# Packed attention feeding a soft mixture of experts on one core: a right-hand work space taken over early by five weight loads, one small product on another engine, and a rewritten order table

## The chip, the cores and the metric

One core of one Trainium2 chip runs the whole program. The metric is device time in microseconds (us), and less is better. Three runs of the kernel before took 237.82, 238.25 and 238.55 us; the median is 238.25 us.

## The reference, cut to what matters

```python
def sm_attn(qq, kk, vv):                       # scale = 1/sqrt(64)
    s = scale * (qq @ kk.T);  a = exp(s - max(s));  a = a / (sum(a) + 1e-9)
    return a @ vv
p_packed = sm_attn(p, k, v)                    # 32 packed rows read 576 keys, for each of 8 x 8 heads
out = sm_attn(q, p_packed, p_packed)           # 576 queries read the 32 packed rows
x = out.transpose(0, 2, 1, 3).reshape(4608, 512)
logits = x @ phi                               # 32 slots = 8 experts x 4
d = softmax(logits, over the 4608 rows)
slot_input = d.T @ x
slot_out[e] = relu(slot_input[e] @ w1[e]) @ w2[e]      # w1 512 x 1024, w2 1024 x 512, 8 experts
c = softmax(logits, over the 32 slots)
result = c @ slot_out                          # 4608 x 512, float32
```

All inputs are float32: q, k and v have 9.4 MB each, w1 and w2 16.8 MB each, p 0.5 MB, and the output 9.4 MB.

## The kernel before

The attention runs in eight steps (i = 0 to 7). A step takes two batches and four heads; two steps make a pair (dd = 0 to 3). In a step, VectorE transposes k (`kt`), TensorE makes the first scores (`s1`), VectorE takes their maximum (`mx1`) and ScalarE their exponential (`e1`). TensorE transposes the result (`ap`) and multiplies it with v (`m`); ScalarE and VectorE scale that (`ppa`, `pp`), and TensorE transposes the packed rows (`pt`). Meanwhile TensorE has transposed q (`qp`, copied out by `qc`) and now makes the second scores in two halves (`s2`, of 36 products each). VectorE takes their maximum and subtracts it (`mx2`, `sb`), ScalarE takes the exponential (`e2`), GpSimd sums and normalises (`z2`, `n2`), and TensorE transposes (`a2p`, copied out by `a2c`).

After each pair the logits follow (`lg`), and a running softmax over all rows: their maximum per slot (`f1` to `f4`), the exponential with its sum `zg` (`f5`, ScalarE), a transpose of that (`fd`, VectorE), `rw`, which is the 128x32 tile `rep` times `zg` (`f_rw`, L701, VectorE), the sum over partitions as a TensorE product with `rw` (`f6`, L706), the running sum `z_run` (`gz`), and the slots' weighted sum of the attention's output (`gr`, `rt`, `gt`, `rb`, `gs`, `sa`). `fl` (L696) keeps the logits for the end.

All of this is issued in the order of a table written out by hand, `ORDER`: each word names one piece, its step, its part, and after `@` the bank of the matmul accumulator (PSUM) and after `:` the engine of a copy. Each engine works through its own instructions in that order.

Loads go through one SyncE queue into a ring of 15.7 MB (`ring`, L129): `pump` (L151) issues the next load when its place is free, and `release` frees a place after the last reader. First p, then k, q, v of each step, then 32 MB of weights, in pieces of 1 MB. The work tiles of the attention lie in two pools, `dpool` on the left and `wpool` on the right. The word `late.0.0`, after the second scores of step 7, closes `wpool` and puts tiles of the last stage there (`f_late`, L797): `xz`, `hT`, `cT`, `identr`.

Then come the experts: `layer1a` (L861) multiplies the slots with w1 and releases each 1 MB piece after use, `layer2` (L917) does it with w2. Between them stand `cq` and `cp` (L933 to L951): nine groups of four transposes that bring the softmax over slots, split in two halves, into `cT`. After the last of them come the last expert (`last2`, L996), its sum, and the output: 36 products of `cT` with the slots' result, copied out by ScalarE and VectorE and stored.

## Time and profile before

| what | value |
|---|---|
| median of 3 runs | 238.25 us |
| the profiled execution | 237.79 us, span 236.0 us, mean granted clock 0.874 |
| TensorE busy | 182.5 us, 77% |
| VectorE busy | 126.1 us, 53% |
| ScalarE, GpSimd busy | 92.8 us, 47.4 us |
| HBM read and written | 62.46 MB, 9.44 MB |
| chain that ended last | TensorE 46%, DMA 17%, VectorE 17%, ScalarE 8% of the span |

Two lines of the page show the stages, in 40 slices of 5.9 us; a digit is the busy share in tenths:

```profile
PE   0987989999799995999997577899959655989000
...
DMA  7999999999999999922919000099999998019997
```

The DMA line is full for some 100 us (q, k, v and the first weights), nearly empty from about 130 to 153 us (the end of the attention), full again to 200 us (the rest of the weights), empty for 10 us, and full at the end (the output). TensorE is nearly full up to 88 us and has its loosest stretches where the DMA line is empty and where weights are awaited. A share of the whole span says little here; each stage has its own limit.

### The profile page before, as it was taken

How to read it: one execution, taken by the hardware profiler on the slowest of the kernel's cores; microseconds unless marked ns; L12 is line 12 of the kernel's file. 1: busy time of each engine (PE TensorE's matmuls, PEld its weight loads, DVE VectorE, ACT ScalarE, POOL GpSimd, SP SyncE). 2: the span in 40 equal slices, each digit the busy share in tenths (PEclk: the TensorE clock that was granted, in tenths of full speed). 3: DMA queues.
4: the chain of work that ended last, by engine and by line, in shares of the span. 5: the costliest groups of instructions: out<-in, count | busy, mean ns of one | idle time of the engine just before them, and what ended most of it. 6: DMA issues, size and time to landing. Idle time of an engine off the chain costs nothing.

```text
span 236.0 us, 6352 instructions
## 1 busy us (share of the span) xinstructions
PE 182.5 (77%) x2715; PEld 117.0 (50%) x2715; DVE 126.1 (53%) x248; ACT 92.8 (39%) x228; POOL 47.4 (20%) x76
## 2 busy tenths in 40 slices
PE   0987989999799995999997577899959655989000
PEld 0665858777496773486866533423311111457000
DVE  1785769676872886464757942772133022159200
ACT  0073847657568574347673422011100000059300
POOL 8100071535305344005458200000000000000000
PEclk9999999999999997799999675579995996599755
DMA  7999999999999999922919000099999998019997
GB/s 161 383 392 391 390 391 390 390 387 391 391 392 388 405 406 403 406 90 60 417 62 350 13 0 0 3 330 431 422 418 422 422 422 332 6 59 409 416 416 301
DMA packets 24683, 72.29 MB, mean 306 GB/s; under 512 B 4176, under 2 KB 4432, under 8 KB 22736
## 3 DMA queue, kind: packets, MB, share of 16 engines
q1 hardware_dynamic: 24080, 71.83, 79.0%
q8 instruction: 21, 0.34, 0.6%
q10 hardware_dynamic: 576, 0.07, 0.2%
q14 instruction: 6, 0.05, 0.1%
HBM read 62.46 MB, written 9.44 MB: 305 GB/s over the span
## 4 chain that ended last, share of the span: by engine, by line
PE 46%; DMA 17%; DVE 17%; ACT 8%; issue 2%; POOL 1%; POOLq 1%; ACTq 0%; DVEq 0%; SPq 0%
DMA ring<-in_moe_w_dram 15%; PE ps L355 6%; PE ps L408 5%; PE ps L868 4%; PE ps L498 4%; PE ps L526 4%; PE ps L1049 3%; PE ps L734 3%; PE ps L607 3%; DVE rw L701 3%; PE ps L386 3%; DVE kT L341 2%; ACT a L369 2%; DMA ring<-in_p_dram 2%; DVE a L557 2%
## 5 line engine op out<-in xcount | busy, mean ns | idle before, releaser
L920 PE MATMUL ps<-ring,hT 128*32 128x512 f32 x112 | 17.7, 722 | 9.4 <-DMA ring<-in_moe_w_dram 9.4
L583 POOL TENSOR_TENSOR zt<-a 128x576 f32<-128x576 f32 x7 | 9.9, 1408 | 72.2 <-ACT a L575 72.2
L341 DVE STREAM_TRANSPOSE kT<-ring 128x576 f32<-128x576 f32 x32 | 23.2, 754 | 1.0 <-DMA ring<-in_k_dram 1.0
L498 PE MATMUL ps<-ident,ring 128*128 128x128 f32 x144 | 20.4, 279 | 0.0
L526 PE MATMUL ps<-ppT,qT 128*64 128x64 f32 x576 | 18.5, 223 | 0.3 <-ACT mm L291 0.3
L598 POOL TENSOR_TENSOR a<-a,zs 128x1152 f32<-128x1152 f32 (+1 forms) x8 | 16.2, 2020 | 12.3 <-DVE zs L594 10.6
L291 ACT COPY qT<-ps 128x512 f32<-128x512 f32 (+1 forms) x43 | 17.9, 477 | 1.7 <-PE ps L498 1.3
L408 PE MATMUL ps<-ring,a1T 64*64 64x128 f32 x576 | 18.2, 272 | 0.3 <-ACT a1T L291 0.3
L291 ACT CAST cT<-ps 128x512 fp32r<-128x512 f32 x6 | 3.5, 586 | 37.1 <-PE ps L946 37.1
L526 PEld LDWEIGHTS ps<-ppT,qT 128*64 128x64 f32 x576 | 17.5, 138 | 0.7 <-ACT mm L291 0.4
L408 PEld LDWEIGHTS ps<-ring,a1T 64*64 64x64 f32 x576 | 15.8, 133 | 2.7 <-DVE rz L421 0.8
L868 PE MATMUL ps<-ring,xz 128*32 128x512 f32 x128 | 16.7, 678 | 0.4 <-DVE xz L953 0.4
L498 PEld LDWEIGHTS ps<-ident,ring 128*128 128x128 f32 x144 | 15.7, 141 | 2.5 <-issue 1.3
L355 PE MATMUL ps<-kT,pT 32*32 32x288 f32 x512 | 16.4, 446 | 0.7 <-issue 0.4
L366 DVE TENSOR_REDUCE nm<-ps 128x2 f32<-128x1152 f32 x8 | 10.9, 1356 | 10.3 <-PE ps L355 8.7
L549 DVE TENSOR_REDUCE mx<-ps 128x36 f32<-128x1152 f32 (+1 forms) x9 | 12.8, 1421 | 4.5 <-PE ps L526 3.4
L369 ACT ACTIVATE a<-ps,nm 128x576 f32<-128x576 f32 x16 | 11.8, 743 | 6.7 <-DVE nm L366 6.7
L607 PE MATMUL ps<-ident,a 128*128 128x128 f32 x72 | 11.9, 303 | 2.8 <-POOL a L598 1.4
L295 DVE CAST cT<-ps 128x512 fp32r<-128x512 f32 x3 | 2.1, 692 | 21.3 <-PE ps L946 21.3
L291 ACT COPY a1T<-ps 128x384 f32<-128x384 f32 x24 | 10.1, 487 | 6.3 <-PE ps L386 6.3
L291 ACT COPY a2T<-ps 128x384 f32<-128x384 f32 x23 | 10.0, 484 | 4.0 <-PE ps L607 4.0
L586 POOL TENSOR_TENSOR zt<-zt 128x288 f32<-128x288 f32 (+2 forms) x21 | 11.2, 535 | 1.6
(130 smaller groups left out, 286.1 us busy)
## 6 DMA issues: line engine op xcount, KB each, us to landing
ring<-in_moe_w_dram SPq DMA_DIRECT2D x31, 1024.0 KB, 13.7
ring<-in_k_dram SPq DMA_DIRECT2D x16, 576.0 KB, 11.9
ring<-in_q_dram SPq DMA_DIRECT2D x16, 576.0 KB, 11.9
ring<-in_v_dram SPq DMA_DIRECT2D x16, 576.0 KB, 12.0
out_dram<-ring SPq DMA_DIRECT2D x10, 768.0 KB, 8.3
ring<-in_moe_w_dram SPq DMA_DIRECT2D x2, 512.0 KB, 18.0
out_dram<-ring SPq DMA_DIRECT2D x2, 512.0 KB, 3.8
ring<-in_p_dram SPq DMA_DIRECT2D x1, 512.0 KB, 4.3
```

Of the source, the lines that this page charges most:

```text
L291: nc.scalar.copy(dst, src)
L341: nc.vector.transpose(kT[:, b2, :, c].rearrange("p m (t r) -> p m t r", t=T), view(f"k{i}.{b2}").rearrange("p (m t c d) -> p m t c d", m=2 ...
L355: nc.tensor.matmul(ps[32 * y : 32 * y + 32, z, 0 : 32 * T], pT[rs, dd, m, b2, g, c], kT[rs, b2, m, c], start=(c == 0), stop=(c == 1),)
L369: nc.scalar.activation(a1[:, :, x].rearrange("p t (h r) -> p h t r", h=2), s1v[:, x].rearrange("p h (t r) -> p h t r", t=T), AF.Exp, bias= ...
L408: nc.tensor.matmul(ps[64 * b2 : 64 * b2 + 64, b + x, 0:P].rearrange("p (m d) -> p m d", m=2), a1T[rs, t, b2], view(f"v{i}.{b2}").rearrange ...
L498: nc.tensor.transpose(ps[:, bank, o : o + P], view(f"q{i}.{b2}")[:, P * y : P * y + P], ident)
L526: nc.tensor.matmul(psf[64 * b2 : 64 * b2 + 64, o : o + 2 * NS].rearrange("p (u s) -> p u s", u=2), qT[:, b2, n, 64 * x : 64 * x + 64], col ...
L549: nc.vector.tensor_reduce(part(mxs[i % 2], c), s2v(i, c), axis=AX.X, op=ALU.max)
L598: (nc.vector if eng == "v" else nc.gpsimd).tensor_tensor(a, a, z.unsqueeze(3).broadcast_to([P, a.shape[1], a.shape[2], NS]), op=ALU.mult)
L607: nc.tensor.transpose(ps[:, bank, o : o + P], a2s[i // NG % 2][:, t, i % NG].rearrange("p c s -> p (c s)"), ident,)
L868: nc.tensor.matmul(ps[32 * a : 32 * a + 32, b + nh, :], xzf[:, (4 * e + a) * NSLOT : (4 * e + a + 1) * NSLOT], wv[:, j, nh * 512 : (nh + 1 ...
L920: nc.tensor.matmul(ps[32 * a : 32 * a + 32, SO, :], hTf[:, (NJ * e + j) * NSLOT : (NJ * e + j + 1) * NSLOT], w2v(e, j), start=(e == 0 and ...
```

## The change

The program makes these changes together:

- **Right-hand space.** `a2_0` and the two `ppT` tiles move from `dpool` to `wpool`. `late` now allocates `xz` and five tiles `ext` of 1 MB there, and issues the next five weight loads into them at once. `hT` and `identr` are made later in the left-hand space; `cT` takes the space of `ext` after `layer2(1)`.
- **Order of the experts.** All nine `cp` groups follow `layer2(1)`; from `layer2(2)` to `layer2(5)` two groups stand behind each expert, and none behind the last.
- **`rw`.** The VectorE product L701 goes; ScalarE makes it in `f_f5`, behind the exponential.
- **Head.** p is loaded in four quarters, the first ahead of k and the others behind k of step 0. GpSimd makes `sel` before the other constants, and a first exponential on ScalarE stands ahead of everything.
- **Second scores.** Each half has its own pair of banks; maximum and subtraction are made by halves in every step.
- **`gt`.** Its four products become eight, each over half the columns.
- **`ORDER`** is rewritten as a whole.

```diff
-mm.7.0:a s2.7.0@0 f5.2.0 n2.6.0:p fd.2.0 rw.2.0 s2.7.1 late.0.0
+f6.2.0 s2.7.1@4 mx2.7.1 gz.2.0 a2p.6.2@6 mx2.7.2 a2p.6.1@1 a2c.6.2:a
...
-    loads.append(("p", B * NG * D, p.rearrange("b (g h) s d -> (h s) (b g) d", g=NG)))
+    loads.append(("p0", 2 * NG * D, rows_p(0)))
     for i in range(NSTEP):
         for b2 in range(2):
             loads.append((f"k{i}.{b2}", 2 * T * D, rows9(k, i, b2)))
+        if i == 0:
+            for dd in range(1, ND):
+                loads.append((f"p{dd}", 2 * NG * D, rows_p(dd)))
...
+    first = const.tile([P, 1], F32, name="first")
+    nc.scalar.activation(first, ones[:, 0:1], AF.Exp)
...
-    a2s = [dpool.tile([P, T, NG, 4, NS], F32, name=f"a2_{x}") for x in range(2)]
+    a2s = [wpool.tile([P, T, NG, 4, NS], F32, name="a2_0"), a2_1]
...
-    ppTs = [dpool.tile([P, 2, 2, 4, NS], F32, name=f"ppT_{x}") for x in range(2)]
+    ppTs = [wpool.tile([P, 2, 2, 4, NS], F32, name=f"ppT_{x}") for x in range(2)]
...
-        if ("s2", i) not in banks:
-            banks["s2", i] = bank
-        b = 512 * banks["s2", i] + x * 2 * T * NS
+        if bank is not None:
+            banks["s2", i, x] = 512 * bank
+        else:
+            banks["s2", i, x] = banks["s2", i, 0] + 2 * T * NS
+        b = banks["s2", i, x]
...
+        nc.scalar.mul(rw, rep[:, 0], zg)
         if dd > 0:
             nc.scalar.activation(al, ps[:, b, W2 : W2 + NSLOT], AF.Exp)
...
-    def f_rw(dd, j, bank, eng):
-        nc.vector.tensor_scalar_mul(rw, rep[:, 0], zg)
...
         for a in range(4):
-            o = 2 * P + a * NSLOT
-            nc.tensor.matmul(
-                ps[:, b, o : o + NSLOT],
-                rt[:, a].rearrange("p b w s -> p (b w s)"),
+            for b2 in range(2):
+                o = 2 * P + a * NSLOT
+                nc.tensor.matmul(
+                    ps[64 * b2 : 64 * b2 + 64, b, o : o + NSLOT],
+                    rt[:, a, b2].rearrange("p w s -> p (w s)"),
...
-        hT = late.tile([P, E, NJ * NSLOT + SPE], F32, name="hT")
-        nc.gpsimd.memset(hT, 0.0)
-        cT = late.tile([P, NT, P], F32R, name="cT")
...
+        ext = [extp.tile([P, 2 * FF], F32, name=f"ext_{x}") for x in range(NEXT)]
...
+        for x in range(NEXT):
+            key, width, src = loads[state["next"]]
+            where[key] = (ext[x], width)
+            load(ext[x][:, 0:width], src)
+            state["next"] += 1
...
+    layer2(1)
+
+    ees.close()
+    lastp = ctx.enter_context(
+        tc.tile_pool(name="lastp", bufs=1, side="right", reuse_waits="tile")
+    )
+    cT = lastp.tile([P, NT, P], F32R, name="cT")
+    cp(0, "a")
+    for e in range(2, E - 1):
+        for n in range(2):
+            t0 = 8 * (e - 2) + 4 * n
+            if t0 + 4 < NT:
+                cq(t0 + 4)
         layer2(e)
+        for n in range(2):
+            t0 = 8 * (e - 2) + 4 * n
+            if t0 + 4 < NT:
+                cp(t0 + 4, "av"[n])
```

Three places in the order of the engines show what moves. Lines are those of each program; a row reads line, operation, output, inputs and shape.

The first place is the softmax over the rows after the second pair. On VectorE before, with `d` the transposed exponential, `zs` the sums that GpSimd normalises with, and `z_run` the running sum:

```order
L593 TENSOR_SCALAR zs_169<-zs_169 128x36
L594 RECIPROCAL zs_169<-zs_169 128x36
L691 STREAM_TRANSPOSE d<-rt 128x288
L701 TENSOR_SCALAR rw<-rep,zg 128x32
L714 TENSOR_TENSOR z_run<-z_run,al 128x32
L715 TENSOR_TENSOR z_run<-z_run,ps 128x32
```

and on ScalarE now:

```order
L320 COPY ppT_160<-ps 64x4x64 x2
L696 ACTIVATE nmg<-ps 128x1
L697 ACTIVATE rt,zg<-ps,nmg 128x288
L705 ACTIVATE rw<-rep,zg 128x32
L707 ACTIVATE al<-ps 128x32
```

The product left VectorE, where it stood behind the sums' reciprocal and the transpose, and stands right behind the exponential that makes `zg`.

The second place is TensorE at the same point. Before, `m` with its number and `dm` are the maximum and its step, `kT` the keys of step 5 and `a` the second attention's weights:

```order
L665 MATMUL ps<-ones,m_175 128x1
L673 MATMUL ps<-dm,ones 128x32
L498 MATMUL ps<-ident,ring 128x128 x4
L450 MATMUL ps<-ident,pp_147 128x128 x2
L498 MATMUL ps<-ident,ring 128x128 x2
L706 MATMUL ps<-rw,ones 128x32
L355 MATMUL ps<-kT,pT 32x288 x32
```

and now, where L542 are the second scores and L750 the weighted sum over rows:

```order
L683 MATMUL ps<-ones,m_185 128x1
L691 MATMUL ps<-dm,ones 128x32
L464 MATMUL ps<-ident,pp_157 128x128 x2
L542 MATMUL ps<-ppT_160,qT 64x64 x18
L722 MATMUL ps<-rw,ones 128x32
L486 MATMUL ps<-phi_sb,ppT_160 64x32 x4
L486 MATMUL ps<-phi_sb,ppT_161 64x32 x4
L542 MATMUL ps<-ppT_160,qT 64x64 x18
L750 MATMUL ps<-a_1_108,d 32x256 x18
```

The product with `rw` had eight transposes between it and the maximum's product; now half of a step's second scores stands there.

The third place is the SyncE queue of loads, around the last weights that are issued before the experts begin. Before:

```order
L167 DMA ring_73<-in_moe_w1_dram 128x2x1024 [waits DMAHW1_49,DVE_49,PE_49]
L167 DMA ring_73<-in_moe_w1_dram 128x2x1024 [waits DMAHW2_49,PE_49]
L167 DMA ring_73<-in_moe_w1_dram 128x2x1024 [waits DMAHW3_49,PE_49]
L167 DMA ring_73<-in_moe_w1_dram 128x2x1024 [waits DMAHW4_49,PE_49]
L167 DMA ring_73<-in_moe_w2_dram 128x2048 [waits DMAHW5_49,PE_49]
```

and now:

```order
L157 DMA ring_73<-in_moe_w1_dram 128x2x1024 [waits DMAHW5_49,PE_49]
L157 DMA ext_0_1891<-in_moe_w1_dram 128x2x1024 [waits DMAHW6_49,Activation_49]
L157 DMA ext_1_1892<-in_moe_w1_dram 128x2x1024 [waits DMAHW7_49,Activation_49]
L157 DMA ext_2_1893<-in_moe_w2_dram 128x2048 [waits DVE_49,DMAHW0_49,PE_49,Activation_49]
L157 DMA ext_3_1894<-in_moe_w2_dram 128x2048 [waits DMAHW1_49,PE_49,Pool_49]
L157 DMA ext_4_1895<-in_moe_w2_dram 128x2048 [waits DMAHW2_49]
L157 DMA ring_73<-in_moe_w2_dram 128x2048 [waits DMAHW3_49,PE_49]
```

In both programs 14 weight loads of 1 MB go into the ring before the experts. Then, before, the queue waits for `layer1a` to release a piece, with 18 MB to go; now five loads go to `ext`, waiting for the last readers and writers of the attention's tiles there, and 13 MB are left to wait for `layer1a`.

## Rows read from the trace of the kernel before

**Rows 1.** Two stretches: busy us (instructions) by engine, PEclk, DMA share, GB/s.

```profile
148.00:150.00 2.00, 1.41 (x12) 1.28 (x13) 0.91 (x4) 0.00 (x0) 0.00 (x0) 0.50 0.00 0
194.00:196.00 2.00, 1.06 (x8) 0.16 (x8) 0.00 (x0) 0.00 (x0) 0.00 (x0) 1.00 1.02 426
```

**Rows 2.** The chain that ended last: start, us, what.

```profile
176.86 19.83 DMA ring<-in_moe_w_dram
```

**Rows 3.** Timeline, experts: start, us, engine, line, instructions, [idle before <- releaser].

```profile
150.83 13.03 PE L868 MATMUL ps<-ring,xz 128*32 128x512 f32 x96 [0.45 <-DVE xz L953]
152.78 31.88 SPq L167 DMA_DIRECT2D ring<-in_moe_w_dram  x19
194.24 1.06 PE L920 MATMUL ps<-ring,hT 128*32 128x512 f32 x8 [0.95 <-DMA ring<-in_moe_w_dram]
196.73 1.86 PE L920 MATMUL ps<-ring,hT 128*32 128x512 f32 x8 [1.43 <-DMA ring<-in_moe_w_dram]
207.36 0.42 DVE L1015 COPY sos<-ps 128x256 f32<-128x256 f32 x1 [5.97 <-PE ps L997]
```

**Rows 4.** Timeline around L701, and line L423's view (ns min/median/max).

```profile
89.47 0.19 ACT L688 ACTIVATE al<-ps 128x32 f32<-128x32 f32 x1
90.20 2.12 POOL L598 TENSOR_TENSOR a<-a,zs 128x1152 f32<-128x1152 f32 x1 [0.77 <-DVE zs L594]
90.32 2.04 DVE L701 TENSOR_SCALAR rw<-rep,zg 128x32 f32<-128x32 f32 x1
...
125.96 3.45 DVE L701 TENSOR_SCALAR rw<-rep,zg 128x32 f32<-128x32 f32 x1
126.76 2.66 DVE L549 TENSOR_REDUCE mx<-ps 128x18 f32<-128x576 f32 x1
130.15 0.75 DVE L549 TENSOR_REDUCE mx<-ps 128x18 f32<-128x576 f32 x1
140.16 0.47 DVE L696 STREAM_TRANSPOSE L_sb<-ps 128x288 f32<-128x288 f32 x1
143.54 0.20 DVE L701 TENSOR_SCALAR rw<-rep,zg 128x32 f32<-128x32 f32 x1
...
L423 DVE TENSOR_TENSOR rzm<-rz,rm x8: 161/162/1059, 17.0 to 118.2; 128x4 f32<-128x4 f32 x8
```

**Rows 5.** TensorE's timeline, first and second pair's softmax over the rows.

```profile
60.05 1.60 PE L355 MATMUL ps<-kT,pT 32*32 32x288 f32 x64
62.84 0.38 PE L706 MATMUL ps<-rw,ones 128*128 128x32 f32 x2 [0.84 <-DVE rw L701]
63.15 1.49 PE L734 MATMUL ps<-a,d 64*32 64x256 f32 x36
92.51 0.60 PE L706 MATMUL ps<-rw,ones 128*128 128x32 f32 x2 [2.79 <-DVE z_run L714]
93.04 2.59 PE L355 MATMUL ps<-kT,pT 32*32 32x288 f32 x64
95.56 2.60 PE L734 MATMUL ps<-a,d 64*32 64x256 f32 x36
```

**Rows 6.** The head: the chain's first load, VectorE's second step, TensorE's second step.

```profile
0.74 4.35 DMA ring<-in_p_dram
...
19.61 0.78 DVE L341 STREAM_TRANSPOSE kT<-ring 128x576 f32<-128x576 f32 x1 [0.72 <-DMA ring<-in_k_dram]
...
21.72 1.60 PE L355 MATMUL ps<-kT,pT 32*32 32x288 f32 x64
```

**Rows 7.** The waits view of TensorE, 11.7 to 127 us: us in total, times, longest.

```profile
PE ps L450 <- DVE pp L437: 2.2, 4, 1.1
```

**Rows 8.** The timeline of the last expert's products.

```profile
201.58 1.94 PE L997 MATMUL ps<-ring,hT 128*32 128x256 f32 x16
203.45 2.08 PE L1010 MATMUL ps<-sot,rep 128*128 128x256 f32 x4
```

**Rows 9.** The timeline: one of the nine groups of transposes between the experts.

```profile
187.79 0.53 PE L946 MATMUL ps<-identr,c 128*128 128x128 f32 x4
```

More of the change, by code (lines that the diff above doesn't have):

```diff
@@ L15 @@
 RING = 30 * 4096
+NEXT = 5
 ORDER = """
[L20 to L26 removed]
@@ new lines @@
+lg.2.0@7 ppa.7.1 z2.6.0:p ppa.7.0 pp.7.1 qp.7.4@6 pp.7.0 f1.2.0
+qp.7.0@3 qc.7.4:a f2.2.0 qp.7.3@2 qc.7.0:v qp.7.1@6 qc.7.3:a f3.2.0
+qp.7.5@3 qp.7.2@1 pt.7.0 qc.7.1:a qc.7.5:a qc.7.2:a ptc.7.1:v ptc.7.0:a
+f4.2.0 rc.6.0 mp.7.0 f5.2.0 s2.7.0@2 n2.6.0:p mm.7.0:v fd.2.0
+f6.2.0 s2.7.1@4 mx2.7.1 gz.2.0 a2p.6.2@6 mx2.7.2 a2p.6.1@1 a2c.6.2:a
+a2p.6.0@0 sb.7.1 a2c.6.1:a a2c.6.0:a gr.2.0@2 late.0.0 sb.7.2 fl.2.0
+e2.7.3 e2.7.4 z2.7.3:v rt.2.1:a rt.2.0:a rc.7.3 gt.2.0 z2.7.4:v
+n2.7.3:p rc.7.4 rb.2.0 n2.7.4:v gs.2.0 a2p.7.0@7 sa.2.0 a2p.7.1@6
@@ L144, in view, with load @@
     def view(key):
-        off, width = where[key]
-        return ring[:, off : off + width]
+        place, width = where[key]
+        return ring[:, place : place + width] if isinstance(place, int) else place[:, 0:width]
+    def load(dst, src):
+        shape = src.shape[1:]
+        if len(shape) == 2:
+            dst = dst.rearrange("p (a b) -> p a b", a=shape[0])
+        elif len(shape) == 3:
+            dst = dst.rearrange("p (a b c) -> p a b c", a=shape[0], b=shape[1])
+        nc.sync.dma_start(out=dst, in_=src)
     def free(off, width):
@@ L160, in pump @@
             where[key] = (off, width)
-            dst = ring[:, off : off + width]
-            shape = src.shape[1:]
-            if len(shape) == 2:
-                dst = dst.rearrange("p (a b) -> p a b", a=shape[0])
-            elif len(shape) == 3:
-                dst = dst.rearrange("p (a b c) -> p a b c", a=shape[0], b=shape[1])
-            nc.sync.dma_start(out=dst, in_=src)
+            load(ring[:, off : off + width], src)
             state["next"] += 1
@@ L535, in s2v @@
     def s2v(i, c):
-        o = 512 * banks["s2", i]
+        o = banks["s2", i, 0 if c != 2 else 1]
+        if c in (1, 2):
+            return psf[:, o : o + 2 * T * NS].rearrange("p (a t s) -> p a t s", a=2, t=T)
         f = psf[:, o : o + 4 * T * NS].rearrange("p (a t s) -> p a t s", a=4, t=T)
@@ L751, in f_gt, with f_w @@
         for a in range(4):
-            o = 2 * P + a * NSLOT
-            nc.tensor.matmul(
-                ps[:, b, o : o + NSLOT],
-                rt[:, a].rearrange("p b w s -> p (b w s)"),
-                rep[:, 0],
-                start=True,
-                stop=True,
-            )
+            for b2 in range(2):
[3 more added lines that the diff above has]
+                    rt[:, a, b2].rearrange("p w s -> p (w s)"),
+                    rep[:, 0],
+                    start=True,
+                    stop=True,
+                )
+    def f_w(n, j, bank, eng):
+        for _ in range(n):
+            nc.tensor.transpose(ps[:, bank, 0:P], ident, ident)
     def f_rb(dd, j, bank, eng):
```

187 lines of the change are left out of this document (87 added, 100 removed).

## The prediction

> **What bounds the kernel now.** I read the chain of waits first, then the windows, then the timeline of each stage. The chain says which stage ends on what: in its last stretch before the output it is one DMA piece of 19.83 us, a load of weights [rows 2]. The windows say what else those stages could use: from 148 to 150 us, at the end of the attention, the DMA engines move nothing and TensorE's granted clock is 0.50, the lower of its two levels (1.2 GHz); from 194 to 196 us the DMA share is 1.02, the clock is 1.00 and TensorE works for 1.06 of 2 us [rows 1]. So there are three stages with different limits: the attention up to 150.83 us, a chain through all compute engines; the experts from there to the end of the last expert's products at 207.36 us, limited by loads [rows 3]; and the rest to 236.0 us, 28.64 us, limited by the stores of the output.
>
> **Stage 2, the five loads.** The queue issues its next weights 1.95 us after the first expert's product (152.78 against 150.83), and 19 loads follow, 17 of 1 MB and two of half that [rows 3]. The sixteenth lets the product at 196.73 start; the one before it stands at 194.24, so a piece takes 2.49 us, and 196.73 - 152.78 - 16 x 2.49 = 4.1 us lie ahead of the first [rows 3]. Five pieces less leave 13 MB: 1.95 + 4.1 + 13 x 2.49 = 38.4 us after the start of stage 2. What hides the five loads is the end of the attention: from the last step's second scores (their maximum starts at 126.76 [rows 4]) to 150.83 are 24 us, in which the DMA engines have nearly nothing else, and five pieces need 12.5 us. If that cover were gone, they would come back at 2.49 us each. On SyncE's queue they stand ahead only of loads that must wait for the experts anyway, so their own waits for the attention's tiles hold up nobody.
>
> Behind the last load come products. At the lower clock the halves of the last expert take 1.94 us each, with 2.08 between them [rows 8]. The twelfth piece lands at 38.4 - 2.5 = 35.9; 35.9 + 1.94 + 2.08 + 1.94 = 41.9 us. At the upper clock each of these halves, and the load sets the end: 38.4 + 0.5 = 38.9. Eight records took 1.06 us at 194.24 and 1.86 at 196.73 after the same kind of wait [rows 3], so both levels occur; I take the middle, 40.4 us, and keep both ends. Before, this stage took 207.36 - 150.83 = 56.5 us: the gain is 16.1.
>
> TensorE has to keep pace: 128 records of w1 at 13.03/96 are 17.4 us, seven experts' w2 at twice 1.06 are 14.8 [rows 3], and nine groups of transposes at 0.53 are 4.8 [rows 9], together 37.0, against 38.4 for the loads. The groups cost nothing as long as that holds; it is close, and it is a rival below.
>
> **Stage 1, the product on ScalarE.** In the second pair the VectorE product started at 90.32 and took 2.04 us; GpSimd's normalisation started at 90.20, took 2.12, and the two end within 0.04 us of each other [rows 4]. In the third pair the product took 3.45, in the fourth, with GpSimd idle, 0.20 [rows 4]. So it is held until GpSimd is done. TensorE waited for it 0.84 us in the first pair and 2.79 in the second, and came out of the second wait at half its pace: 2.59 instead of 1.60 us for the scores, 2.60 instead of 1.49 for the weighted sum [rows 5]. In the third pair the maximum behind it took 2.66 us instead of 0.75 [rows 4], on the chain that ends the attention. Together 0.84 + 2.79 + 0.99 + 1.11 + 1.91 = 7.6 us. A ScalarE operation of the same shape takes 0.19 [rows 4], three of them 0.6: the gain is 7.0 if the product's own wait is not replaced. Next late is `zg` itself, and half of a step's second scores now stands between on TensorE.
>
> Against this move speaks a sentence of the Trainium skill, page Perfetto Trace Analysis, section Optimizing Scalar/DVE Operations: "If a DVE performance mode (2x or 4x) is available, it will be faster". By that sentence alone the move gains nothing and the sum below is 218.0; the rows have 0.20 against 0.19 us alone and 2.04 to 3.45 beside GpSimd, so by them it is 211.0. (The same section warns of a port that GpSimd and VectorE share, and with that the rows agree.)
>
> **Stage 1, the head.** The first load takes 4.35 us on the chain, and a quarter of it now goes ahead; that bounds the gain from above at three quarters, 3.3 us. But the k of step 1 keeps its place in the queue: VectorE waits for it until 19.61, two transposes of 0.78 follow, and the scores that need them start at 21.72 [rows 6], so at that point only 21.72 - 21.17 = 0.55 us can be gained. Step 2 is less tied to its loads. I take the middle, 1.9. The early exponential loads ScalarE's table beside the first load: nothing.
>
> **Stage 1, the rest of the order.** TensorE waits 2.2 us for the scaled packed rows before transposing them [rows 7]; now the next step's scores, 1.60 us long [rows 5], stand ahead of that transpose in several steps. Between 0 and 2.2 I take 1.5. The transpose of the logits (0.47, on the last pair's chain between two maxima [rows 4]) moves behind: 0.5. The second scores' maxima by halves take 0.75 each [rows 4]; a half can start earlier, and an extra instruction can be in the way. Either is worth at most 0.75 us in each of seven steps, so between 5.3 gained and 5.3 lost; I take nothing, since VectorE is busy about half of the time. The eight products of `gt` load as many columns as the four did: nothing; if eight more records cost 0.19 each, half of the 0.38 for two [rows 5], 1.5 in the last pair, where nothing covers them. The other edits move no work onto the path.
>
> Sum for stage 1: 7.0 + 1.9 + 1.5 + 0.5 = 10.9 us; the experts start at 139.9.
>
> **Sum.** 139.9 + 40.4 + 28.6 = 208.9 us of span. The profiled execution has 237.79 - 236.0 = 1.8 us around its span: 210.7. It lies 0.46 us under the median of the runs shown, so on that scale I forecast 211.1, and say 211.0 us.
>
> **The rivals.**
>
> - **The hold passes on.** GpSimd's normalisation still runs beside VectorE, and the operations behind the departed product stay there. For this: L423, two small tiles multiplied, took 1.06 us at its worst and 0.16 in the median [rows 4], so L701 is not the only one that is held. Against it: in the new order GpSimd's normalisation is mostly over when the running sum is formed. If all of the 7.0 us and the 1.5 of the transposes come back, 219.5. The Trainium skill, SBUF - State Buffer, section SBUF: two separate sides, has a rule for this: a VectorE operation with two inputs in SBUF is held while GpSimd reads SBUF; the row of L423 agrees.
> - **TensorE becomes the bound of the experts.** Its 37.0 us above are at 1.06 us for eight records; at 1.86, seven experts take 26.0 instead of 14.8 us [rows 3]. If half of them run so, 5.6 us: 216.6. It decides once TensorE needs more than about 40 us. For it: the clock fell at 196.73. Against: TensorE would wait less between pieces than now.
> - **The loads do not come early.** If the tiles' last readers come late or the queue is behind, all five fall into stage 2: 12.4 us, 223.4. Against: 24 us are free for 12.5 us of loads.
> - **The other side: a wait in every step.** Place: the second scores, whose halves now have bank pairs of their own, which transposes must leave. Price: if TensorE runs dry there as at 92.51, it loses 2.79 us and then 2.1 us at the lower clock [rows 5], 4.9 us a step. From six steps on (6 x 4.9 = 29) the gain of 27 is gone; in all eight it would be 39 lost, and the kernel at 250. Against: the maxima take 0.75 a half, and other work of TensorE stands between.
>
> **How the numbers follow.** The forecast gets 0.60, with a range of its own from 206.5 to 217: 1.4 + 0.7 + 1.5 below (head, transposes, clock) and 1.4 + 1.5 + 1.5 + 1.5 above (with `gt`). The hold passes on: 0.18. TensorE the bound: 0.13. Loads late: 0.05. A wait in every step: 0.02. The remaining 0.02 is for halves that gain up to 5.3, to 205.7. The range from 205.5 to 218.5 takes in the forecast, TensorE as the bound, and a hold that comes back in part; it leaves out the full return, late loads and the last rival. A measurement of this kernel can tell 0.3%, about 0.7 us, from no change. Faster 0.97, the same 0.01, slower 0.02.
>
> **What would show it.** Right: the loads into `ext` start near the end of step 7's second scores and land before the first w1 product; 14 loads follow that product, at 2.5 us per MB; the DMA line has no empty stretch of 20 us before the experts; `rw` takes 0.2 us in all four pairs and TensorE's wait for L706's successor is gone; the first w1 product starts near 140 us and the span after the last expert is still 28 to 29 us. Wrong: that product starts after 145 us; loads into `ext` land behind it; w2 products that start without waiting for a load; TensorE at clock 0.5 in the middle of the attention.

## The result, and the profile after

The changed kernel takes **216.66 us** (median of 4 runs, 214.71 to 218.41) against 238.03 us for the kernel before on the same chip: a ratio of 0.9035, with a 95% interval from 0.899 to 0.908. Forecast were 211.0 us, between 205.5 and 218.5. The sign and the range held; the forecast was 5.7 us too low. Ratios and intervals, here and below, come from undisturbed executions alone, so a ratio need not be the quotient of two medians. The profiled execution, the fastest of the four, took 214.71 us, 212.9 of them span, against 210.7 and 208.9 forecast for it.

The three stages show where: the attention up to the first w1 product, the experts up to the copy of the last expert's products, and the rest.

| stage | before | forecast | after |
|---|---|---|---|
| attention, to the first w1 product | 150.83 | 139.9 | 146.47 |
| experts, from there to the copy (L1015, now L1050) | 56.5 | 40.4 | 37.6 |
| the rest | 28.6 | 28.6 | 28.8 |

The page of the changed kernel:

```profile
span 212.9 us, 6420 instructions
...
PE 167.8 (79%) x2747; PEld 112.9 (53%) x2747; DVE 136.1 (64%) x286; ACT 85.2 (40%) x206; POOL 47.4 (22%) x75
...
PEclk9999999999999999999999999679999999999655
DMA  6999999999999999669919799941999999169996
...
q8 instruction: 21, 0.34, 0.7%
...
PE 47%; DMA 17%; DVE 14%; ACT 8%; issue 5%; SPq 0%; ACTq 0%; DVEq 0%
```

The stretch of nearly 25 us in which the DMA line was empty before the experts has shrunk to two slices of 5.3 us (digits 4 and 1). VectorE is busier (64% against 53%). And 5% of the chain of waits is now "issue", time for which the profile shows no other cause.

SyncE's queue in the timeline of the changed kernel answers to the 19 loads of [rows 3]:

```profile
122.94 7.31 SPq L157 DMA_DIRECT2D ext<-in_moe_w_dram  x5
147.55 18.82 SPq L157 DMA_DIRECT2D ring<-in_moe_w_dram  x14
```

The five loads go out while the attention's last step drains, and 14 instead of 19 follow the first w1 product, 1.08 us behind it. By the trace's DMA packets the five have landed by 142.4 us, 4 us ahead of that product. On the chain of waits the stretch before the output, against the one DMA piece of [rows 2], is now:

```profile
146.47 3.67 PE ps L889 x32
150.14 9.83 DMA ring<-in_moe_w_dram
160.03 20.84 DMA ring<-in_moe_w_dram
180.91 1.07 PE ps L1032 x16
```

TensorE's timeline around both ends of the experts, and VectorE's copy there:

```profile
140.40 0.41 PE L722 MATMUL ps<-rw,ones 128*128 128x32 f32 x2 [1.32 <-ACT al L707]
...
144.39 0.66 PE L770 MATMUL ps<-rep,rt 128*64 128x32 f32 x16 [0.93 <-DVE rt L324]
...
146.47 1.08 PE L889 MATMUL ps<-ring,xz 128*32 128x512 f32 x8 [0.45 <-DVE xz L974]
...
178.42 1.07 PE L941 MATMUL ps<-ring,hT 128*32 128x512 f32 x8 [0.81 <-DMA ring<-in_moe_w_dram]
180.91 1.07 PE L1032 MATMUL ps<-ring,hT 128*32 128x256 f32 x16 [1.43 <-DMA ring<-in_moe_w_dram]
```

```profile
184.09 0.42 DVE L1050 COPY sos<-ps 128x256 f32<-128x256 f32 x1 [3.85 <-PE ps L1032]
```

TensorE waits for weights at two places only, at 178.42 and 180.91. The windows of the experts (columns: the stretch; us busy and records of PE, PEld, DVE, ACT and POOL; granted clock; DMA share; GB/s) say why:

```profile
146.50:160.00 13.50, 13.50 (x132) 4.81 (x136) 7.90 (x12) 1.75 (x2) 0.00 (x0) 1.00 0.86 340
160.00:170.00 10.00, 10.00 (x98) 3.87 (x88) 4.82 (x16) 1.76 (x3) 0.00 (x0) 1.00 1.02 423
170.00:184.00 14.00, 11.59 (x107) 4.59 (x105) 5.87 (x17) 1.76 (x3) 0.00 (x0) 1.00 0.85 348
```

TensorE is busy for 35.1 of 37.5 us at the upper level of its clock, 2.4 GHz (granted clock 1.00); it ends at 184.05, and the last weights land at 182.9 us by the trace's DMA packets. Both limits are met within 1.2 us of each other. [rows 1] had a clock of 0.50 at 148 us.

The waits of TensorE from 6 to 146.4 us (us in total, times, longest), against [rows 4, 5, 7]:

```profile
PE ps L422 <- issue: 4.4, 3, 2.2
PE ps L802 <- DVE rb L786: 2.3, 2, 1.8
PE ps L770 <- DVE rt L324: 1.8, 2, 0.9
PE ps L369 <- DVE kT L355: 1.5, 2, 1.0
PE ps L722 <- ACT al L707: 1.3, 1, 1.3
...
PE ps L369 <- issue: 0.8, 1, 0.8
...
PE ps L542 <- issue: 0.2, 1, 0.2
```

The waits for `rw`, for `d` and for the scaled packed rows `pp`, which the forecast wanted gone, are gone. But **5.4 us of "issue"** stand at the top; the kernel before had 0.44 us. TensorE's timeline has them in the middle of rows of equal products:

```profile
28.10 0.54 PE L422 MATMUL ps<-ring,a1T 64*64 64x128 f32 x9
30.10 1.97 PE L422 MATMUL ps<-ring,a1T 64*64 64x128 f32 x63 [1.47 <-issue]
...
36.56 0.72 PE L369 MATMUL ps<-kT,pT 32*32 32x288 f32 x16 [0.82 <-issue]
...
46.30 0.87 PE L422 MATMUL ps<-ring,a1T 64*64 64x128 f32 x20
49.32 0.43 PE L422 MATMUL ps<-ring,a1T 64*64 64x128 f32 x4 [2.15 <-issue]
```

No semaphore is awaited there. The trace also records every transfer of queue q8, which the page calls "instruction": 21 of them, 0.34 MB, so 16 KB each. Counting all records of TensorE's queue (weight loads, products and 41 semaphore and drain instructions) from zero, the waits stand 256 records or a multiple of that apart, at 193 + 256 k, and each ends 1.2 to 1.5 us after the k-th transfer of q8 has landed:

```
 k   transfer of q8, us   wait before record   TensorE goes on, us   wait, us
 2     27.73 to 28.82             705                30.10             1.47
 3     33.95 to 35.04             961                36.56             0.82
 5     46.76 to 47.88            1473                49.32             2.15
13     97.94 to 98.92            3521               100.16             0.23
14    106.58 to 107.69           3777               109.14             0.82
```

So q8 brings TensorE's instructions, 256 at a time, and TensorE at times runs out of them. That is **theory A** of the experiments: freed time cannot be used where the next block of instructions is not there yet. From 27 to 92 us, with the DMA engines full, these transfers came 4.9 us apart or more in every kernel that loads all of q, k and v, mostly 6.1 to 6.5. The fetch of block k is not made long ahead: in the changed kernel, for k from 3 to 12, it started 2.7 to 3.9 us after TensorE had begun the block before, at record 193 + 256 (k - 1). The rivals are **B**, VectorE has become the bound of the attention, and **C**, GpSimd or ScalarE hands its hold on.

### The profile page after: what moved, and what is told of

Same layout as the page of the kernel before. It is cut to its first block, busy times and chain, and to the rows that moved or that the text cites. A ratio compares the mean times of both kernels' runs of the same rounds, so it can differ in the third digit from the quotient of the medians.

```text
span 212.9 us, 6420 instructions
## 1 busy us (share of the span) xinstructions
PE 167.8 (79%) x2747; PEld 112.9 (53%) x2747; DVE 136.1 (64%) x286; ACT 85.2 (40%) x206; POOL 47.4 (22%) x75
## 4 chain that ended last, share of the span: by engine, by line
PE 47%; DMA 17%; DVE 14%; ACT 8%; issue 5%; SPq 0%; ACTq 0%; DVEq 0%
DMA ring<-in_moe_w_dram 14%; PE ps L422 7%; PE ps L542 7%; PE ps L369 6%; PE ps L512 6%; PE ps L400 4%; ACT ring L320 3%; DVE a L575 3%; PE ps L625 3%; DMA ring<-in_k_dram 3%; DVE mx L567 2%; PE ps L335 2%; PE ps L750 2%; PE ps L889 2%; ACT a L593 2%
## 5 line engine op out<-in xcount | busy, mean ns | idle before, releaser
L422 PE MATMUL ps<-ring,a1T 64*64 64x128 f32 x576 | 19.7, 274 | 4.4 <-issue 4.4
L542 PE MATMUL ps<-ppT,qT 128*64 128x64 f32 x576 | 20.1, 224 | 2.2 <-ACT ppT L320 1.0
L542 PEld LDWEIGHTS ps<-ppT,qT 128*64 128x64 f32 x576 | 18.2, 138 | 4.1 <-issue 2.7
L369 PE MATMUL ps<-kT,pT 32*32 32x288 f32 x512 | 16.3, 446 | 2.3 <-DVE kT L355 1.5
L567 DVE TENSOR_REDUCE mx<-ps 128x18 f32<-128x576 f32 x16 | 11.9, 746 | 5.5 <-PE ps L542 5.5
L320 ACT COPY qT<-ps 128x512 f32<-128x512 f32 (+1 forms) x32 | 14.0, 486 | 3.6 <-PE ps L512 3.5
L380 DVE TENSOR_REDUCE nm<-ps 128x2 f32<-128x1152 f32 x8 | 10.9, 1358 | 6.1 <-PE ps L369 6.1
L889 PE MATMUL ps<-ring,xz 128*32 128x512 f32 x112 | 12.5, 593 | 0.4 <-DVE xz L974 0.4
L575 DVE TENSOR_TENSOR a<-ps,mx 128x576 f32<-128x576 f32 x16 | 11.9, 754 | 0.3
L593 ACT ACTIVATE a<-a 128x1152 f32<-128x1152 f32 (+2 forms) x9 | 9.5, 1062 | 6.5 <-DVE a L575 6.5
L369 PEld LDWEIGHTS ps<-kT,pT 32*32 32x32 f32 x512 | 7.3, 107 | 8.2 <-issue 2.8
L941 PE MATMUL ps<-ring,hT 128*32 128x512 f32 x88 | 10.9, 599 | 0.8 <-DMA ring<-in_moe_w_dram 0.8
L400 PE MATMUL ps<-ident,a 128*128 128x128 f32 x72 | 10.0, 277 | 1.1 <-ACT a2T L320 0.7
```

Source lines behind the costliest of these rows:

```text
L320: nc.scalar.copy(dst, src)
L369: nc.tensor.matmul(ps[32 * y : 32 * y + 32, z, 0 : 32 * T], pT[rs, dd, m, b2, g, c], kT[rs, b2, m, c], start=(c == 0), stop=(c == 1),)
L400: nc.tensor.transpose(ps[:, bank, o : o + P], a1[:, t].rearrange("p x r -> p (x r)"), ident)
L422: nc.tensor.matmul(ps[64 * b2 : 64 * b2 + 64, b + x, 0:P].rearrange("p (m d) -> p m d", m=2), a1T[rs, t, b2], view(f"v{i}.{b2}").rearrange ...
L542: nc.tensor.matmul(psf[64 * b2 : 64 * b2 + 64, o : o + 2 * NS].rearrange("p (u s) -> p u s", u=2), qT[:, b2, n, 64 * x : 64 * x + 64], col ...
L567: nc.vector.tensor_reduce(part(mxs[i % 2], c), s2v(i, c), axis=AX.X, op=ALU.max)
```

## The experiments

The times below belong to single profiled executions and are for the first w1 product, the experts, and the sum of the "issue" waits; the medians and ratios (to the kernel before on the same chip) come from all runs. One more execution of the unchanged new kernel (the last experiment) gives 147.24 and 40.87 us where the first gave 146.47 and 37.62; differences under 1 us in the attention, or under 3 us in the experts, are not read as effects. The same program has the ratios 0.904 and 0.923 in two series of runs, with intervals that do not meet, so ratios of different series are not compared more closely than that. The kernels with product and loads, with the head added, with `gt` whole and the whole change once more ran in one series, on one chip.

| kernel | first w1 | experts | issue | median | ratio (95%) |
|---|---|---|---|---|---|
| before | 150.83 | 56.5 | 0.4 | | |
| before, product on ScalarE | 144.95 | 54.8 | 1.1 | 229.67 | 0.965 (0.957 to 0.973) |
| product and loads | 146.16 | 41.5 | 1.3 | 217.28 | 0.919 (0.907 to 0.931) |
| product, loads, head | 148.60 | 39.3 | 1.3 | 217.79 | 0.925 (0.919 to 0.932) |
| whole change | 146.47 | 37.6 | 5.4 | 216.66 | 0.904 (0.899 to 0.908) |
| whole change, once more | 147.24 | 40.9 | 3.9 | 216.81 | 0.923 (0.914 to 0.931) |
| without the product's move | 151.32 | 39.5 | 5.0 | 221.07 | 0.930 (0.923 to 0.937) |
| without the early loads | 146.32 | 53.9 | 4.6 | 232.65 | 0.977 (0.969 to 0.985) |
| with the old order | 150.81 | 41.1 | 3.1 | 221.89 | 0.943 (0.934 to 0.952) |
| with gt whole | 149.98 | 40.3 | 3.2 | 219.80 | 0.933 (0.922 to 0.943) |

### The product alone, and the change without it

To the kernel before, in `f_f5` behind the exponential (`f_rw` does nothing):

```diff
+        nc.scalar.mul(rw, rep[:, 0], zg)
```

> The kernel before with one part of the change: rw's product goes to ScalarE, right behind the exponential of its pair; order, head and loads are as before. The prediction's sum gives this part 7.0 us (median 231.0, four waits of TensorE on L706 gone). Theory A (up to some 90 us TensorE is held by its instruction fetch, because the loads fill the DMA engines, so time freed there comes back as a wait called issue): the waits of pairs 0 and 1 lie in that stretch and their 3.6 us are given back, so about 3.4 us are left, median 234.6. Theory B (VectorE has become the bound of the attention): a product less on VectorE shows whole, 7 us or more, 231 or under.

To the changed kernel, out of `f_f5` and into `f_fd` behind the transpose:

```diff
-        nc.scalar.mul(rw, rep[:, 0], zg)
+        nc.vector.tensor_scalar_mul(rw, rep[:, 0], zg)
```

> The changed kernel with rw's product back on VectorE, behind the transpose of d; all else as changed. The prediction's sum: 7.0 us slower, median 223.7. Theory A: pairs 0 and 1 cost little, since TensorE has issue waits there anyway; about 3.4 us slower or less, 218 to 220. Theory B: 7 us slower or more.

Alone on the kernel before, the move brings the first w1 product 5.9 us earlier and the median to 229.67 us. Taken out of the whole change it costs 4.1 to 4.9 us at that place (against the two executions of the unchanged kernel), and the median is 221.07 us. The prediction's 7.0 was near. Theory A, as stated for the first of these runs, was not: the wait of pair 1 did not come back, and the median is the one that B gave (231 or under); the second lies between A and B. In the second run the product on VectorE is held once only, 1.45 us in the third pair against 0.19 to 0.22 in the others, and TensorE waits for it 2.2 us in all; what the rest of the 4.1 to 4.9 us is was not settled. The instructions of `rw` and of VectorE in pair 1, in the kernel with the product alone (the first row: ns min, median and max, first and last start):

```profile
L687 ACT ACTIVATE rw<-rep,zg x4: 321/322/324, 62.2 to 138.3; 128x32 f32<-128x32 f32 x4
```

```profile
90.50 0.42 DVE L692 STREAM_TRANSPOSE d<-rt 128x288 f32<-128x288 f32 x1
90.84 2.06 DVE L715 TENSOR_TENSOR z_run<-z_run,al 128x32 f32<-128x32 f32 x1
93.00 0.19 DVE L716 TENSOR_TENSOR z_run<-z_run,ps 128x32 f32<-128x32 f32 x1
```

ScalarE takes 0.32 us in all four pairs. VectorE's next operation with operands in SBUF is held instead, 2.06 us beside GpSimd's normalisation (90.72 to 92.84): the rival "the hold passes on" happens in this kernel once. It did not cost the gain, since TensorE does not wait for `z_run` as it did for `rw`. In the whole change no operation of VectorE on such small tiles takes more than 1.13 us (a copy of 128x128, at 62.37).

### The five loads

To the changed kernel:

```diff
-NEXT = 5
+NEXT = 0
```

> The changed kernel without the five early loads (their number set to 0; the places of the other tensors stay). The prediction's sum: the loads are worth 12.4 us of the experts, so about 229. Rival: the loads carry all of the 18.9 us by which the experts got shorter, so 235.6. Both leave the attention's end (first w1 product) where it is, near 146.5; if it moves, loads and attention meet.

The attention ends where it did (146.32), and the experts take 53.9 instead of 37.6 to 40.9 us: the loads are worth 13.0 to 16.3 us in the profiles, 16 in the medians, between the two expectations. TensorE's waits from 146 to 201 us in this kernel:

```profile
PE ps L941 <- DMA ring<-in_moe_w_dram: 9.0, 9, 1.4
PE ps L1032 <- DMA ring<-in_moe_w_dram: 1.0, 1, 1.0
```

Ten waits for weights, against two with the loads. In between, TensorE's clock falls. The windows of the same kernel:

```profile
170.00:180.00 10.00, 7.15 (x52) 2.57 (x56) 2.81 (x9) 1.17 (x2) 0.00 (x0) 0.83 1.01 421
...
190.00:200.20 10.20, 7.78 (x52) 2.45 (x44) 0.69 (x1) 0.00 (x0) 0.00 (x0) 0.67 0.54 220
```

### Is the late fetch caused by the loads?

Three kernels change the loads of q, k and v and nothing that TensorE does. The first holds at most two steps' loads in the ring (in `pump`):

```diff
+AHEAD = 12
...
+            if key[0] in "kqv" and sum(r[0][0] in "kqv" for r in regions) >= AHEAD:
+                return
```

> The changed kernel, with at most 12 loads of q, k and v (two steps) held in the ring at a time, so that these loads follow the work instead of filling the DMA engines up to 90 us. Theory A: the fetches of TensorE's instructions come in time, its issue waits of about 5 us between 28 and 110 us go, and the first w1 product comes 3 to 6 us earlier (140.5 to 143.5 instead of 146.5), median 211 to 214. Theory B (VectorE is the bound) and theory C (GpSimd or ScalarE hands its hold on): no earlier than 146 us, median 216 to 217, or later if loads are missed.

The second makes each load of q, k and v in two halves (in `load`):

```diff
-        nc.sync.dma_start(out=dst, in_=src)
+        if src.shape[-1] == T * D:
+            c = T * D // 2
+            for y in range(2):
+                nc.sync.dma_start(out=dst[:, :, y * c : y * c + c], in_=src[:, :, y * c : y * c + c])
+        else:
+            nc.sync.dma_start(out=dst, in_=src)
```

> The changed kernel with each load of q, k and v as two DMAs of half the columns (pieces of 1152 B instead of 2304 B), a remedy if a fetch waits behind pieces of loads. Theory A with that mechanism: fetches come about 5 us apart instead of 6.2, issue waits fall from 5.4 us to under 2.5, first w1 product at 143 to 144.5 us, median 213 to 215. If the fetch waits behind bytes or behind its own latency, nothing moves: 146.5 and 216 to 217.

Neither helped: first w1 product at 147.38 and 149.45 us, issue waits 4.1 and 4.2, medians 218.03 us (ratio 0.916, 0.909 to 0.923) and 220.82 us (0.940, 0.930 to 0.950). The first did not do what it was meant to: q, k and v landed 12.0 us after their issue as before, and the DMA line stayed full. The second moved 357 GB/s where the whole loads move 390, and the fetches came no closer. For k from 3 to 12 they started 3.05 us on average after TensorE had begun the block before, against 3.45 us in the changed kernel, so halving the pieces does not halve a fetch's wait; for the rest these two decide nothing.

The third takes the loads away, of the changed kernel and of the one before. Steps 2 to 7 go from the list of loads and read the places of steps 0 and 1, which are not released before the end:

```diff
+        return key[0] + str(int(key[1]) % 2) + key[2:] if key[0] in "kqv" else key
...
+            if key[0] == "w" and state.get("used", 0) < 30:
+                return
...
```

> The changed kernel, but steps 2 to 7 read the q, k and v of steps 0 and 1 again and load nothing (their data is left out), and the weights' loads wait until 30 of the 48 pieces are used up, so that the DMA engines are idle from about 20 us to 90 us while the instructions stay the same. Theory A (instruction fetches of TensorE stand behind the loads): the issue waits of 5.4 us go to under 1 us from 25 us on, fetches come less than 6 us apart where TensorE asks for them, and the first w1 product comes at about 141 to 142.5 us. Theory B (VectorE is the bound): waits on VectorE take their place and the first w1 product stays at 145.5 to 146.5 us.

> The same edit on the kernel before: steps 2 to 7 read the q, k and v of steps 0 and 1 again, no loads between about 20 and 90 us. It has 0.44 us of issue waits, so theory A expects 0.4 to 1 us: first w1 product at 150 to 150.4 us instead of 150.83. If it comes 3 us earlier or more, then the loads cost both kernels something besides the fetch (VectorE's and ScalarE's accesses, or TensorE's own).

The page of the changed kernel with this edit, and two rows of TensorE's timeline:

```profile
DMA  6999999800000005000587699704999997069996
```

```profile
30.12 1.97 PE L436 MATMUL ps<-ring,a1T 64*64 64x128 f32 x63 [1.47 <-issue]
...
36.30 0.72 PE L383 MATMUL ps<-kT,pT 32*32 32x288 f32 x16 [0.55 <-issue]
```

The ring still fills up to about 43 us, so the first two waits are there. From then on the DMA engines are idle, and **no issue wait is left**: the 2.15 us at 49 us and the two behind 97 us are gone. The starts of the fetches (us), and the time at which TensorE began the block before each, tell the same:

```
                          k = 3      4      5      6      7
changed kernel          33.95  40.37  46.76  53.08  60.51
  block before begun    30.10  36.56  42.93  49.32  57.61
without the loads       33.88  40.00  43.57  47.32  55.11
  block before begun    30.12  36.30  42.47  46.54  54.78
```

Beside full DMA engines a fetch starts 2.7 to 3.9 us after the block before it is begun (k from 3 to 12), with idle engines at most 1.1 us after (k from 5 to 13). How far apart the fetches then come is TensorE's own pace: 3.6 and 3.8 us where it catches up, 7.8 us at k = 7. The first w1 product comes at 143.91 us, 2.6 us earlier, of 3.2 us of issue waits removed; that is between the two expectations. At the `gt` products of the third pair it is 3.8 us ahead (126.63 against 130.41 us); 1.2 us of that are lost in the last pair, where its granted clock is 0.50 for 11.1 us up to the first w1 product, against 6.8 us. B and C are out as the cause: VectorE, ScalarE and GpSimd have the same work in both. On the kernel before, the same edit moves that place by 0.7 us (150.16; ratio 0.999, 0.993 to 1.005), as A expects of a kernel with hardly any such wait. (The median of the first, 215.66 us, is not comparable: its weights come later, and its experts take 41.6 us.)

The waits can cost more than their own time. In the changed kernel's second execution the clock falls 2.0 us after the wait that ends at 48.55 us, and stays down for 6.8 us:

```profile
50.60:57.40 6.80, 6.16 (x45) 5.54 (x49) 3.69 (x9) 4.52 (x13) 0.00 (x0) 0.50 1.05 388
```

From that wait's end to the second scores behind it are 9.66 us, against 6.96 us in the first execution, whose clock stayed at 1.00: 2.7 us. In five of the seven executions with this order and all loads the granted clock falls to 0.50 within 3 us of such a wait, for 3.4 to 6.8 us; the other two have waits as long without it.

### The order and the head

To the changed kernel, the whole order list of before (without `rw`, and with `late.0.0` behind `gr.2.0`):

```diff
-p.0.0 px.0.0@7 kt.0.0 pc.0.0:a kt.0.1 kt.0.2 kt.0.3 p.1.0
...
+p.0.0 p.1.0 px.0.0@7 p.2.0 p.3.0 px.1.0@6 pc.0.0:v kt.0.0 kt.0.1
...
```

> The changed kernel (product on ScalarE, p in four loads, the five early loads, the tensors' new places) with the order list of before; only rw's step is gone from it and the early loads stand behind the last sums of pair 2. Theory A (the new order packs TensorE's instructions so that its instruction fetch is late three to four times, 5.4 us of issue waits): under the old order these waits are about 1 us, and the first w1 product comes at 143 to 145 us as with the product alone on ScalarE (144.95), against 146.5 under the new order; experts 37.6 us, median 213 to 215. Rival (the 5.4 us missing are lost to the new code or the places of the tensors, whatever the order): first w1 product at 148 or later, median 218 or more.

The first w1 product came at 150.81 us: the number of the rival. But the two tables don't differ alone here. The old one asks for all four quarters of p before the first scores, and three of them now arrive behind k; the first scores start at 14.79 us, not at 11.74. So I added to the kernel before only the product, and the loads with the tiles' new places and the order of the experts that goes with them:

```diff
+NEXT = 5
...
+        nc.scalar.mul(rw, rep[:, 0], zg)
...
+        ext = [extp.tile([P, 2 * FF], F32, name=f"ext_{x}") for x in range(NEXT)]
```

and to that kernel the new head alone:

```diff
-p.0.0 p.1.0 px.0.0@7 p.2.0 p.3.0 px.1.0@6 pc.0.0:v kt.0.0 kt.0.1
+p.0.0 px.0.0@7 kt.0.0 pc.0.0:a kt.0.1 kt.0.2 kt.0.3 p.1.0 s1.0.0@0
...
-    loads.append(("p", B * NG * D, p.rearrange("b (g h) s d -> (h s) (b g) d", g=NG)))
+    loads.append(("p0", 2 * NG * D, rows_p(0)))
```

> The kernel before with two parts of the change: the product on ScalarE, and the five early loads with the tensors' new places; order (but for rw's step, and the early loads behind pair 2's last sums), head, p in one load and gt's four products stay as before. If parts add up: first w1 product at 144.95 us as with the product alone, experts 37.6 to 40, 28.7 behind: span 211.3 to 213.7, median 213 to 216, as fast as the whole change or up to 2 us faster; that says the new order and head bring nothing, because their gain comes back as issue waits. If the order is worth the 3.9 us of the prediction, this kernel is 3 to 4 us slower than the whole change, 219 to 221.

> The kernel of the run with product and loads, plus the new head (p in four loads, sel and the first exponential earlier, the first scores ahead of the other p); the order behind the head is that of before. The trace of the changed kernel has the DMA engines full from 2 us on and the first transposes of q at 14.3 us in the new head against 14.0 in the old, so the loads set the head: theory L (loads) expects the q transposes at 13.7 to 14.5 and the first w1 product within 0.7 us of the run without the new head. The prediction's 1.9 us would put it at 143.

Product and loads, with the old order and head, take 217.28 us beside 216.81 us for the whole change on the same chip; the intervals of the ratios overlap nearly whole. The rest of the change, the whole new order and head, brings nothing that can be measured. The median is a little above the 213 to 216 expected, and the first w1 product, at 146.16 us, comes 1.2 us later than with the product alone. The loads are not the cause. GpSimd's fill of `hT`, which the change makes later, now runs beside VectorE's next operation on `z_run`, which took 0.18 us with the product alone:

```profile
141.93 1.83 POOL L963 MEMSET hT<- 128x2080 f32 x1 [12.61 <-PE ps L736]
...
142.54 1.26 DVE L719 TENSOR_SCALAR z_run<-z_run 128x32 f32<-128x32 f32 x1
```

In the whole change that operation comes ahead of the fill (141.07 against 143.68 us) and takes 0.18 us. The head by itself makes the first w1 product 2.4 us later. TensorE's timeline, product and loads without the new head:

```profile
11.72 1.60 PE L355 MATMUL ps<-kT,pT 32*32 32x288 f32 x64
13.25 2.26 PE L498 MATMUL ps<-ident,ring 128*128 128x128 f32 x18
...
21.70 1.60 PE L355 MATMUL ps<-kT,pT 32*32 32x288 f32 x64
```

and with it:

```profile
7.05 1.21 PE L364 MATMUL ps<-kT,pT 32*32 32x288 f32 x16 [1.36 <-DVE kT L350]
...
13.84 0.63 PE L507 MATMUL ps<-ident,ring 128*128 128x128 f32 x4
14.79 1.09 PE L507 MATMUL ps<-ident,ring 128*128 128x128 f32 x8 [0.31 <-DVE pT L319]
15.72 1.03 PE L330 MATMUL ps<-a 128*128 128x256 f32 x4
...
23.36 2.21 PE L364 MATMUL ps<-kT,pT 32*32 32x288 f32 x64
```

The first scores start 4.7 us earlier, but the transposes of q (L498, now L507) not: they came at the time theory L gave. Its other number, no more than 0.7 us at the first w1 product, fails as the prediction's does. The products of p's other quarters (L330) now stand among them, and the second step's scores come 1.7 us later, not earlier. At record 449 TensorE is 2.3 us behind (24.81 against 22.48 us), and so it stays up to the last pair; at the end of the kernel the medians differ by 0.5 us. In the whole change the new order stands behind the head, and there these scores start at 20.65 us, 1.1 us earlier than in the kernel before; the wait for instructions at 30.10 us takes 1.47 us.

### The halves of gt

To the changed kernel, and then the changed kernel as it is:

```diff
-            for b2 in range(2):
...
-                    ps[64 * b2 : 64 * b2 + 64, b, o : o + NSLOT],
-                    rt[:, a, b2].rearrange("p w s -> p (w s)"),
...
+                ps[:, b, o : o + NSLOT],
+                rt[:, a].rearrange("p b w s -> p (b w s)"),
...
```

> The changed kernel with gt's products in one piece again, four in a pair instead of eight, so 32 fewer products and weight loads each pair of which TensorE need not fetch. The prediction puts the halves at nothing, at most 1.5 us in the last pair. Expected: first w1 product 0 to 1.2 us earlier than 146.47; were the number of instructions what counts, the issue waits would fall by a quarter of one fetch, 1.5 us at most.

> The changed kernel once more, as it is, beside the three others on the same chip: 214.7 to 217, first w1 product at 146 to 147, issue waits 4 to 5.5 us.

(In the first expectation the count is wrong: in the trace a product of `gt` is two records with a weight load each, so whole a pair has 16 records less, and all four have 64.) The halves are faster in the last pair, against the expectation: without them the first w1 product comes 2.7 us later, and the median is 219.80 against 216.81 us, though the intervals of the ratios overlap. The last pair, with the halves and without:

```profile
144.50 1.07 PE L770 MATMUL ps<-rep,rt 128*64 128x32 f32 x16 [0.93 <-DVE rt L324]
```

```profile
146.41 1.92 PE L769 MATMUL ps<-rep,rt 128*128 128x32 f32 x8 [0.93 <-DVE rt L324]
```

Both at a granted clock of 0.50: 0.85 us are shown to be the halves' own. Another 1.2 us of the 2.7 is the clock in the profile without them: at 134.86 us its transposes L625 took 2.18 us instead of 1.20, and the products L649 behind them 1.60 instead of 1.33. The rest is under 1 us.

## Why the prediction was right, and where it fell short

**The experts (56.5 to 40.4): right.** 37.6 and 40.9 us in two executions, around the forecast of 40.4 and near its ends of 38.9 and 41.9. The loads went out early, as described, and came in time. The rival that TensorE becomes the bound was close to true: it is busy for 35.1 of 37.5 us, and all but two of the w2 products start without a wait for a load, which the prediction had named as a sign of being wrong. In the profiled execution that cost little, since the clock stayed at the upper level up to the end of the experts. In the second execution part of the first expert and of the last ran at a granted clock of 0.50 (the first half of the last and the sum behind it took 1.66 and 2.08 us instead of 1.07 and 1.13), and the experts took 40.9 us. The two executions lie near the two ends that the forecast gave to the two levels.

**The product on ScalarE (7.0): the mechanism right, the size a little too large.** 5.9 us alone, 4.1 to 4.9 inside the whole change, where only one of the four products on VectorE is held, 1.45 us. An operation takes 0.32 us, not the 0.19 of the exponential [rows 4]. The sentence of the Trainium skill that spoke against the move (page Perfetto Trace Analysis, section Optimizing Scalar/DVE Operations) does not decide here: VectorE's version is quick alone and held beside GpSimd [rows 4].

**The failed step is the sum of stage 1, "7.0 + 1.9 + 1.5 + 0.5 = 10.9 us; the experts start at 139.9".** They started at 146.47: 4.4 us gained. By runs that add one part after another, 150.83 became 144.95 with the product, 146.16 with the loads, 148.60 with the head and 146.47 with the order (147.24 in the second execution), the halves of `gt` among it. So the terms behind the product, forecast as 3.9 us gained, were 1.5 us lost. The prediction's own sign of being wrong, a first w1 product after 145 us, came.

- The head (1.9) was a middle between 0.55 us, which the rows gave for step 1, and 3.3 us, because step 2 was called less tied to its loads. Measured by itself, the head loses 2.4 us: the transposes of q start no earlier, and more work stands among them.
- The waits for `pp` (1.5) went as forecast, from 2.2 us to nothing. For the logits' transpose (0.5), TensorE's wait of 0.97 us in the last pair became 0.65. The halves of `gt`, set at nothing or a loss, gave 0.85 us in the last pair. Yet the runs without and with the new order differ by 2.1 us in all (1.4 against the second execution), of which 1.1 us is the operation on `z_run` that the fill of `hT` no longer holds. The new order has issue waits of 5.4 us (3.9 in the second execution) where the old one has 1.3.
- That the time freed early comes back as a wait for instructions was no rival in the prediction. It is a cause shown for the difference, and not only argued: with the DMA engines idle 3.2 us of these waits vanish and 2.6 us are gained. If the other 2.2 us went at the same rate, the first w1 product would come near 142 us (an estimate). The remaining 2 us to the forecast are not taken apart; product (1.1 to 2.9 us) and head each fell short.
- How little an order could gain while the loads run shows in the kernel with product and loads. TensorE needs 64.4 us for the ten blocks of 256 records from record 705 on (28.71 to 93.13 us), 6.4 us each, and beside the loads the blocks mostly come 6.1 to 6.5 us apart: hardly anything was left there for a new order (an estimate from these numbers).

**The rivals and the range.** A wait in every step did not occur. The hold passed on in the kernel with the product alone, where TensorE did not wait for it, and in the kernels with the loads and the old order, where the fill of `hT` cost 1.1 us of the last pair; in the whole change it cost nothing that shows. A clock of 0.50 in the middle of the attention, named as a sign of being wrong, came in the second execution. The lower end of the forecast's own range, 206.5, does not follow from its terms: 211.0 less 1.4 + 0.7 + 1.5 is 207.4. And a measurement told less than the 0.3% assumed: the four runs lie between 214.71 and 218.41 us.

**What stays open:** why a fetch starts 2.7 to 3.9 us after the block before is begun when the DMA engines are full. Halving the pieces shortened that by 0.4 us on average, and keeping fewer loads in flight was not reached. The loads and the new order of the experts were never taken apart. Whether an order could be found that keeps the early waits away was not tried.

## What to carry to other kernels

Before costing an order that packs an engine more tightly, look at "issue" in its waits and at the instruction queue in the DMA part of the page: a program written out flat has to be fetched, and beside loads that fill the DMA engines the fetch set a pace of its own here, 256 instructions in 6.1 to 6.5 us. Measure each part of a change alone: here a product and five loads carry all of it, and a new head with a new order of several hundred pieces cancels itself. And where the rows already bound a term (0.55 us for the head at the second step), a middle with a bound that they do not show is a guess.

## What the hardware showed that was not expected

- TensorE's instructions come in blocks of 16 KB, 256 at a time, and the k-th block holds what is needed from record 193 + 256 k on; each wait ended 1.2 to 1.5 us after its block had landed. With full DMA engines a block's transfer started 2.7 to 3.9 us after TensorE had begun the block before (k from 3 to 12 in the changed kernel), and blocks came mostly 6.1 to 6.5 us apart; with idle engines it started at most 1.1 us after, and they came as TensorE asked for them, down to 3.6 us apart. The Trainium skill, page Runtime: NRT & Kernel Launch, section Instruction fetch mechanics, has the block of 16 KiB and 256 instructions, and the trace agrees; it calls the crossing mostly hidden, and here the waits were 5.4 us. It also gives TensorE room for 2048 instructions, but TensorE ran dry at the very block whose fetch had just landed.
- After a wait for instructions of 1.5 to 2.2 us the granted clock fell to 0.50 for 3.4 to 6.8 us in some executions and not in others; once that cost 2.7 us.
- GpSimd's fill of a 128x2080 tile (1.83 us) held a VectorE operation on a 128x32 tile for 1.26 us instead of 0.18.
- Eight products with half the columns are faster than four whole ones: 1.07 against 1.92 us at a granted clock of 0.50.
- Loads in pieces of 1152 instead of 2304 B moved 357 instead of 390 GB/s.
